# A fused attention and mixture-of-experts kernel whose start-up is re-ordered: q loaded before k and v, the next batch's keys made earlier, one table loaded sooner

## The chip, the cores and the metric

The kernel runs on one core of a Trainium2 chip. The metric is the device time of one execution in microseconds (us). Executions of one kernel differ by 2 to 3 us out of 990, and that matters here: the whole effect is about 3 us. *Times* come from four to six executions of a kernel (three for the first reading of the kernel before), beside the kernel before on the same chip. *Milestones* come from one profiled execution: they tell where TensorE is at which moment, to a hundredth of a microsecond, but of one execution only.

Engines: PE is TensorE, DVE is VectorE, ACT is ScalarE, POOL is GpSimd, SP the queue engine.

## The reference, cut to what matters

A cosine-weighted linear attention for 8 batches of 576 tokens (8 heads of 64) feeds a mixture of 8 experts with Sinkhorn routing.

```python
q_p, k_p = phi(q), phi(k)                    # relu, times cos and sin of the position: 64 -> 128 features
kv = einsum('bhsf,bhsd->bhfd', k_p, v)       # "key sums"
z = sum(k_p, axis=2)
out = einsum('bhsf,bhfd->bhsd', q_p, kv) / (einsum('bhsf,bhf->bhs', q_p, z) + 1e-6)
# x = out as [4608, 512]; P = sinkhorn(exp(x @ w_gate)), 8 iterations
# result = sum over experts e of P[:, e] * (relu(x @ w1[e]) @ w2[e])
```

Nearly all the work is the expert layers. They need x, so they cannot start before the attention of the first batch is done. That start-up is the subject.

## The kernel before

One batch of attention goes through these steps, four head pairs (`hk`) at a time: load q, k, v (cast to fp16 on the way, by the one queue that POOL feeds); ReLU of k on ACT (`prep_k`); the products with cos and sin on DVE (`k_p`, `q_p`); transposes of `q_p` on PE, with a ReLU on the way out of PSUM (`turn`); key sums on PE (`sums_begun`) and their copies (`sums_made`, which makes `zsel`); `denominators` (24 matmuls, then add, reciprocal and rounding on DVE); and `attend`, which writes `xT`. From batch 2 on the transposes of `q_p` are made by a DMA. Tokens go through the first expert in blocks of 512: block 0 uses batch 0, block 1 needs batch 1 too.

Engines work strictly in the written order here (a helper chains each instruction to the one before it on its engine), so a late operand holds up everything behind it.

```python
        load(0, 0, "kv")
        # ... ident made on POOL
        load(0, 1, "kv")
        load(0, 0, "q")
        load(0, 1, "q")
        w0 = new_weights(wA)
        load_w1(w0, 0, 4)
        load(1, 0, "kv")
        load(1, 1, "kv")
        load(1, 0, "q")
        load(1, 1, "q")
        load_w2(w0, 0, 4)

        def keep_busy(n):            # dummy matmuls, which keep PE's clock up
            for _ in range(n):
                te.matmul(out=idle_ps[:, 0:P], lhsT=ones_sq[:], rhs=ones_sq[:], start=True, stop=True)
        idle_ps = ps_y.tile([P, Dm], FP32, name="y_ps")
        keep_busy(56)
        # ...
        prep_pair(0, 0)                      # relu(k), k_p, copy of v for head pairs 0 and 1
        begun = [sums_begun(0, 0)]
        keep_busy(12)
        prep_pair(0, 1)
        sums_made(0, 0, begun[0])
        prep_q(0, 0)
        begun.append(sums_begun(0, 1))
        keep_busy(12)
        prep_q(0, 1)
        for hk in range(HK):
            for i in range(3):
                turn(0, hk, i, hk < 2 or i == 0)
            keep_busy(8)
            # ... sums_made(0, 1), prep_q(0, hk + 2)
        denominators(0)
        keep_busy(36)
        # ...
        for hk in range(HK):
            attend(0, hk)
            if hk:
                prep_k(1, hk - 1)
            if hk == HK - 1:
                prep_kv(1, 0)
                prep_kv(1, 1)
                prep_k(1, 3)
            # ... block 0's first four w1 products, as xT comes
        prep_kv(1, 2)
        prep_kv(1, 3)

        ahead = (                            # of batch 2, done in block 0's slots 11 to 15
            (prep_k, 0), (prep_q, 0), (prep_k, 1), (prep_kv, 0), (prep_q, 1), (prep_k, 2),
            (prep_kv, 1), (prep_q, 2), (prep_k, 3), (prep_kv, 2),
        )
                # block 0, by slot: sums of batch 1 in 4 and 6, turns in 7 to 10, denominators in 10,
                # gates in 11, attends in 13, 14, 15, 15
```

A block has 16 slots: 8 for w1 products (four matmuls of 512 columns each), 8 for w2 products.

Of the kernel before, what the change touches and what calls it, by code (L numbers as in the profile page):

```python
# [10 lines left out]
FP32 = mybir.dt.float32  # L11
# [4 lines left out]
AF = mybir.ActivationFunctionType  # L16
# [9 lines left out]
def kernel(  # L26
# [18 lines left out]
    HK = H // 2  # L45
# [74 lines left out]
    def new_weights(pool):  # L120
        return pool.tile([P, KT, F], F16, name="w1e"), pool.tile([P, FT, Dm], F16, name="w2e")

    def load_w1(w, e, cuts):
        view = moe_w1[e].rearrange("(kt p) f -> p kt f", p=P)
        for i in range(cuts):
            f0, f1 = i * F // cuts, (i + 1) * F // cuts
            nc.gpsimd.dma_start(out=w[0][:, :, f0:f1], in_=view[:, :, f0:f1])

# [26 lines left out]
    def ffn2(hT, w, c0, g, y_ps, fts):  # L155

        for ft in fts:
            te.matmul(
                out=y_ps,
                lhsT=hT[:, ft, c0 : c0 + P],  # L160
                rhs=w[1][:, ft, :],
                start=(ft == 0),
                stop=(ft == FT - 1),
            )
        if FT - 1 in fts:

            if g % 2 == 0 or TCH // P <= g < (B - 1) * TCH // P:
                se.copy(out=acc(g), in_=y_ps)
            else:
                ve.tensor_copy(out=acc(g), in_=y_ps)  # L170
# [10 lines left out]
    with ExitStack() as p1:  # L181
# [15 lines left out]
        def load(b, half, names="qkv", held_back=False):  # L197
            for name in names:
                x = ld.tile([P, 2, C, D], F16, name=f"{name}_ld")
                view = sources[name][b].rearrange("(hk hh) (p c) d -> (hh p) hk (c d)", hh=2, c=C)  # L200
                i = nc.gpsimd.dma_start(
                    out=x[:].rearrange("p hk c d -> p hk (c d)"),
                    in_=view[:, 2 * half : 2 * half + 2],
                )
                if held_back:

                    after(ve.last, i)
                for i in range(2):
                    loaded[name, b, 2 * half + i] = x[:, i]
# [8 lines left out]
            allow_small_or_imprecise_dtypes=True,  # L218
        )

        load(0, 0, "kv")
        ones_sq = cs_pool.tile([P, P], F16, name="ones_sq")
        ve.memset(ones_sq[:], 1.0)
        ident = cs_pool.tile([P, P], F16, name="ident")
# [1 line left out]
            out=ident[:], in_=ones_sq[:], pattern=[[-1, P]], compare_op=ALU.is_equal,  # L226
            fill=0.0, base=0, channel_multiplier=1,
        )
        load(0, 1, "kv")
        load(0, 0, "q")  # L230
        load(0, 1, "q")
        w0 = new_weights(wA)
        load_w1(w0, 0, 4)
        load(1, 0, "kv")
        load(1, 1, "kv")
        load(1, 0, "q")
        load(1, 1, "q")
        load_w2(w0, 0, 4)
# [7 lines left out]
                )  # L246

        idle_ps = ps_y.tile([P, Dm], FP32, name="y_ps")
        keep_busy(56)

        wrap = cs_pool.tile([P, C], FP32, name="wrap")
        ve.tensor_scalar(
# [9 lines left out]
        s_b = sval[:].unsqueeze(2).to_broadcast([P, C, D])  # L262
        se.activation(out=cs[:, :, 0, :], in_=s_b, func=AF.Sin, bias=half_pi[:], scale=-ang)
        se.activation(out=cs[:, :, 1, :], in_=s_b, func=AF.Sin, scale=ang)


        zmask = held[:, C * 2 * D + 3 * H * D : C * 2 * D + 3 * H * D + H * 32].rearrange("p (h r) -> p h r", h=H)
# [76 lines left out]
                qps[b, hk] = q_p  # L344

        def prep_kv(b, hk, copy=ve.tensor_copy):
            k16, v16 = (loaded.pop((name, b, hk)) for name in "kv")
            k_p = kp_pool.tile([P, C, 2, D], F16, name="k_p")
            ve.tensor_tensor(
                out=k_p[:], in0=k16.unsqueeze(2).to_broadcast([P, C, 2, D]),  # L350
                in1=cs, op=ALU.mult,
            )

            v_aug = v_augs[(b * HK + hk) % len(v_augs)]
            copy(out=v_aug[:, :, 0:D], in_=v16)
            kps[b, hk] = (k_p, v_aug)

        def turn(b, hk, i, scalar=None):

# [45 lines left out]
        def sums_made(b, half, kv_ps):  # L405
            kv_sb, zsel = kvs[b]
            for hh in range(2):
                kv_v = kv_ps[hh][:, 0 : 2 * (D + 1)].rearrange("p (hk d) -> p hk d", d=D + 1)
                se.copy(out=kv_sb[:, 2 * half : 2 * half + 2, hh, :], in_=kv_v[:, :, 0:D])
                ve.tensor_tensor(  # L410
                    out=zsel[:, 4 * half + hh : 4 * half + 4 : 2, :],
                    in0=zmask[:, 4 * half + hh : 4 * half + 4 : 2, :],
                    in1=kv_v[:, :, D : D + 1].to_broadcast([P, 2, 32]),
                    op=ALU.mult,
                )

        def denominators(b):

# [85 lines left out]
        turns = [(hk, i) for hk in range(HK) for i in range(3)]  # L504


        def prep_pair(b, half):
            for hk in (2 * half, 2 * half + 1):
                prep_k(b, hk)
            for hk in (2 * half, 2 * half + 1):  # L510
                prep_kv(b, hk, se.copy)

        prep_pair(0, 0)
        begun = [sums_begun(0, 0)]
        keep_busy(12)
        prep_pair(0, 1)
        sums_made(0, 0, begun[0])
        prep_q(0, 0)
        begun.append(sums_begun(0, 1))
        keep_busy(12)  # L520
        prep_q(0, 1)
        for hk in range(HK):
            for i in range(3):
                turn(0, hk, i, hk < 2 or i == 0)
            keep_busy(8)
            if hk == 0:
                sums_made(0, 1, begun[1])
            if hk < 2:
                prep_q(0, hk + 2)
        denominators(0)  # L530
        keep_busy(36)

        hT = hA.tile([P, FT, TCH], F16, name="hT")
        first_ps = [
# [3 lines left out]
        ]  # L538
        for hk in range(HK):
            attend(0, hk)  # L540
            if hk:
                prep_k(1, hk - 1)
            if hk == HK - 1:
                prep_kv(1, 0)
                prep_kv(1, 1)
                prep_k(1, 3)
            for kt in ((), (0,), (1,), (2, 3))[hk]:
                for ft, h_ps in enumerate(first_ps):
                    te.matmul(
                        out=h_ps[:],  # L550
                        lhsT=w0[0][:, kt, ft * P : (ft + 1) * P],
                        rhs=xT[:, kt, 0:TCH],
                        start=(kt == 0),
                        stop=(kt == KT - 1),
                    )
                    if kt == KT - 1:
                        se.activation(out=hT[:, ft, 0:TCH], in_=h_ps[:], func=AF.Relu)
        prep_kv(1, 2)
        prep_kv(1, 3)

        ahead = (
            (prep_k, 0), (prep_q, 0), (prep_k, 1), (prep_kv, 0), (prep_q, 1), (prep_k, 2),
# [2 lines left out]
        for j in range(B):  # L565
            b = j + 1
            if j == 0:

                at(0, 4, lambda: begun.append(sums_begun(1, 0)))
                at(0, 5, lambda: sums_made(1, 0, begun[2]))  # L570
                at(0, 6, lambda: begun.append(sums_begun(1, 1)))
                at(0, 7, prep_q, 1, 0)
                at(0, 7, prep_q, 1, 1)
                for hk in range(HK):
                    for i in range(3):
                        at(0, 7 + hk, turn, 1, hk, i)
                    if hk == 0:
                        at(0, 7, lambda: sums_made(1, 1, begun[3]))
                    if hk < 2:
                        at(0, 7 + hk, prep_q, 1, hk + 2)  # L580
                at(0, 10, denominators, 1)
                at(0, 11, gates, 0)
                for hk in range(HK):
                    at(0, min(13 + hk, 15), attend, 1, hk)
            elif b < B:
                if j == 1:
                    at(j, 0, prep_q, b, 3)
                    at(j, 1, prep_kv, b, 3)
                    at(j, 1, sums, b, 0)
                    at(j, 3, sums, b, 1)  # L590
                else:
                    at(j, 0, sums, b, 1)
                at(j, 5 if j == 1 else 3, denominators, b)
                for hk in range(HK):
                    at(j, (8 if j == 1 else 6) + 2 * hk, attend, b, hk)
            if j:
                at(j, 5, gates, j)
            if j == 0:
                for half in range(2):
                    at(j, 3, load, b + 1, half)  # L600
                for i, (fn, hk) in enumerate(ahead):
                    at(j, 11 + i // 2, fn, b + 1, hk)
            elif b + 1 < B:
                for slot, fn, hk in (
                    (3, prep_k, 0), (4, prep_q, 0), (4, prep_k, 1), (5, prep_q, 1),
                    (7, prep_kv, 0), (7, prep_k, 2), (7, prep_q, 2), (9, prep_q, 3),
                    (9, prep_k, 3), (9, prep_kv, 1), (11, prep_kv, 2), (13, prep_kv, 3),
                ):
                    at(j, slot + (j == 1), fn, b + 1, hk)
                at(j, 15 if j == 1 else 14, sums, b + 1, 0)  # L610
            if j == 0:
                for half in range(2):
                    at(1, 0, load, b + 2, half)
            elif b + 2 < B:
                for half in range(2):
                    at(j, 11 + half, load, b + 2, half, "qkv", True)
# [524 lines left out]
```

## Time and profile before

990.26 us, the median of three runs (988.73 to 991.0). The profiled execution has a span of 987.4 us, measured from the first to the last instruction.

| reading of the execution before | us |
|---|---|
| last load of batch 0's v lands | 11.16 |
| last load of batch 0's q lands | 14.91 |
| first transpose of batch 0 | 14.35 |
| denominators of batch 0 start | 20.00 |
| first attend | 23.46 |
| block 1 runs with all its operands (the 4th of its w1 matmuls) | 54.29 |
| block 2 starts | 74.52 |

First the page's busy time of PE and its chain of waits, kernel before. "PE 93%" is the share of the span in which the chain that ended last ran on PE.

```profile
PE 968.0 (98%) x7846; PEld 677.9 (69%) x7846; DVE 810.4 (82%) x1838; ACT 566.4 (57%) x1260; POOL 60.4 (6%) x82
...
PE 93%; DMA 2%; DVE 2%; ACT 1%; POOL 1%; issue 0%; DVEq 0%; POOLq 0%; ACTq 0%; SPq 0%
```

PE is the bound, so only a microsecond in which PE idles, or runs dummies, or runs at a low clock, can be won. They lie in the start-up. Next the windows view, kernel before: in each stretch the busy us of each engine with the number of instructions, then the granted PE clock, the DMA share and GB/s.

```profile
10.00:15.00 5.00, 3.51 (x62) 3.31 (x60) 3.15 (x6) 2.61 (x7) 2.08 (x3) 0.57 1.30 199
45.00:50.00 5.00, 4.26 (x30) 2.14 (x29) 4.93 (x12) 2.80 (x8) 0.00 (x0) 1.00 1.27 201
50.00:55.00 5.00, 3.03 (x18) 1.32 (x18) 4.97 (x12) 2.12 (x6) 0.00 (x0) 1.00 0.84 163
```

From 10 to 15 us the clock is 0.57. From 45 to 55 us DVE is full (4.93 and 4.97 of 5) while PE is busy only 4.26 and 3.03. The timeline of PE says what it waits for; the columns are start, us, engine, line, operation, output and inputs, count, and in brackets the idle time before and what ended it.

```profile
14.35 0.85 PE L109 MATMUL small_ps<-ident,q_p 128*128 128x128 f16 x6
...
20.00 0.89 PE L109 MATMUL small_ps<-q_pT,zsel 128*32 128x192 f16 x24
...
23.46 0.42 PE L109 MATMUL small_ps<-hl,acc_hi 96*128 96x192 f16 x3 [0.45 <-DVE hl L109]
...
51.97 0.61 PE L109 MATMUL h_ps<-xT,w1e 128*128 128x512 f16 x2
53.57 0.38 PE L109 MATMUL h_ps<-xT,w1e 128*128 128x512 f16 x1 [0.99 <-DVE xT L109]
54.29 1.24 PE L109 MATMUL h_ps<-xT,w1e 128*128 128x512 f16 x5 [0.35 <-DVE xT L109]
```

Block 1's w1 matmuls come in the order of `xT`'s four parts. The third waits 0.99 us for an `xT`, the fourth 0.35 us: DVE has other work in front of it. One more line, from ACT's timeline, kernel before:

```profile
41.94 1.28 ACT L109 ACT_TABLE_LOAD   x1
```

This is the Exp table, loaded at its first use, in the middle of the busy part.

### The profile page before, as it was taken

To read this page: it belongs to the slowest core of one execution; us is meant where nothing else is said; L and a number is where in the kernel's file an instruction comes from. 1 tells how busy PE (TensorE), PEld (TensorE's weight loads), DVE (VectorE), ACT (ScalarE), POOL (GpSimd) and SP (SyncE) were. 2 spreads that over 40 slices of the span, in tenths; PEclk is the share of its full clock that TensorE was granted. 3 is DMA by queue.
4 is the path that set the end of the run, shared out by engine and by line. 5 is a ranking of instruction groups with operands and counts; after the bars stand their busy time and mean duration, and the time that the engine had idled before them with its cause. 6 is when DMAs were issued, how large, how long until landed. Compare 5 with 4: busy or idle time off the path is not lost.

```text
span 987.4 us, 20228 instructions
## 1 busy us (share of the span) xinstructions
PE 968.0 (98%) x7846; PEld 677.9 (69%) x7846; DVE 810.4 (82%) x1838; ACT 566.4 (57%) x1260; POOL 60.4 (6%) x82
## 2 busy tenths in 40 slices
PE   7999999989999999999999999999999999999997
PEld 6445544447777777777777777777777777777775
DVE  5886774779889888988789888988789888988887
ACT  5756665467776555555555555555555555555551
POOL 6302110010000000000000000000000000000001
PEclk8999999999999999999999999999999999999999
DMA  9969981642013410133113400233103400104535
GB/s 168 206 99 154 160 153 26 125 67 67 26 48 68 75 42 25 38 79 67 42 33 68 88 29 25 51 66 68 49 25 68 92 25 27 48 25 114 131 86 128
DMA packets 80336, 73.54 MB, mean 74 GB/s; under 512 B 33264, under 2 KB 72176, under 8 KB 80240
## 3 DMA queue, kind: packets, MB, share of 16 engines
q0 software_dynamic: 27232, 30.94, 19.9%
q1 hardware_dynamic: 52768, 41.06, 16.9%
q8 instruction: 61, 1.00, 0.4%
q14 instruction: 35, 0.29, 0.1%
q10 hardware_dynamic: 240, 0.26, 0.1%
HBM read 83.12 MB, written 12.98 MB: 97 GB/s over the span
## 4 chain that ended last, share of the span: by engine, by line
PE 93%; DMA 2%; DVE 2%; ACT 1%; POOL 1%; issue 0%; DVEq 0%; POOLq 0%; ACTq 0%; SPq 0%
PE rows_ps L109 34%; PE h_ps L109 28%; PE copied_ps L109 11%; PE p_ps L109 11%; PE y_ps L109 5%; PE small_ps L109 4%; DMA v_ld<-in_v_dram 2%; DMA q_pT<-q_p 1%; DVE xT L109 0%; DVE acc_hi L814 0%; POOL hs_last L829 0%; DVE P_tok L109 0%; DMA out_dram<-acc_lo 0%; DVE colp L109 0%; ACT u L109 0%
## 5 line engine op out<-in xcount | busy, mean ns | idle before, releaser
L814 DVE SCALAR_TENSOR_TENSOR acc_lo<-rows_ps,P_tok,acc_lo 128x512 f32<-128x512 f32 (+1 forms) x322 | 203.7, 642 | 74.5 <-PE rows_ps L109 74.4
L109 PEld LDWEIGHTS <-H 128*128 128x128 f16 x2080 | 203.0, 98 | 83.1 <-issue 1.2
L750 ACT CAST u<-h_ps 128x384 f16<-128x384 f32 x288 | 137.8, 478 | 131.2 <-PE h_ps L109 130.6
L109 PEld LDWEIGHTS <-w1e 128*128 128x128 f16 x1632 | 156.3, 98 | 67.9 <-issue 7.8
L744 DVE CUSTOM_DVE_ANT_0 H<-p_ps,u 128x384 f16<-128x384 f32 x329 | 181.7, 552 | 6.6 <-PE p_ps L109 6.4
L109 PEld LDWEIGHTS <-hs 128*128 128x128 f16 x1500 | 146.6, 98 | 56.2
L109 PE MATMUL h_ps<-S,w1e 128*128 128x384 f16 x672 | 164.1, 326 | 1.1 <-ACT u L109 0.9
L109 PE MATMUL p_ps<-xT,T 128*128 128x384 f16 x672 | 164.1, 326 | 0.1
L109 PE MATMUL h_ps<-xT,w1e 128*128 128x384 f16 (+1 forms) x616 | 150.3, 351 | 1.4 <-DVE xT L109 1.3
L109 PE MATMUL rows_ps<-V,H 128*128 128x256 f16 x1000 | 150.0, 273 | 0.7 <-DVE acc_hi L814 0.7
L109 PE MATMUL rows_ps<-w2e,hs 128*128 128x256 f16 x1000 | 150.0, 273 | 0.0
L782 ACT ACTIVATE H<-h_ps 128x384 f16<-128x384 f32 x144 | 70.7, 491 | 95.0 <-PE h_ps L109 95.0
L109 PEld LDWEIGHTS <-T 128*128 128x128 f16 x1008 | 98.1, 98 | 29.2 <-issue 2.8
L109 PE MATMUL rows_ps<-w2e,H 128*128 128x256 f16 (+1 forms) x568 | 91.2, 285 | 0.0
L763 ACT COPY copied_ps<-h_ps 128x384 f32<-128x384 f32 x144 | 67.5, 468 | 35.2 <-PE h_ps L109 35.2
L773 ACT ACTIVATE H<-copied_ps 128x384 f16<-128x384 f32 x144 | 70.9, 492 | 20.3 <-PE copied_ps L109 20.3
L109 PE MATMUL h_ps<-S,T 128*128 128x384 f16 x336 | 81.8, 325 | 0.3 <-ACT copied_ps L109 0.3
L109 PE MATMUL copied_ps<-xT,w1e 128*128 128x384 f16 x336 | 82.1, 326 | 0.0
L109 PE MATMUL copied_ps<-w2e,H 128*128 128x256 f16 x504 | 75.5, 272 | 0.0
L109 PE MATMUL rows_ps<-V,hs 128*128 128x256 f16 x500 | 75.0, 272 | 0.0
L814 DVE SCALAR_TENSOR_TENSOR acc_lo<-copied_ps,P_tok,acc_lo 128x256 f32<-128x256 f32 x126 | 60.3, 479 | 0.4
L814 DVE SCALAR_TENSOR_TENSOR acc_hi<-rows_ps,P_tok,acc_hi 128x512 f32<-128x512 f32 (+1 forms) x56 | 41.3, 738 | 20.1 <-PE rows_ps L109 19.3
(135 smaller groups left out, 957.5 us busy)
## 6 DMA issues: line engine op xcount, KB each, us to landing
S<-x_saved SPq DMA_DIRECT2D x108, 192.0 KB, 2.4
out_dram<-acc_lo SPq DMA_DIRECT2D x62, 128.0 KB, 2.4
w1e<-in_moe_w_dram POOLq DMA_DIRECT2D x7, 1024.0 KB, 9.3
w2e<-in_moe_w_dram POOLq DMA_DIRECT2D x7, 1024.0 KB, 10.0
k_ld<-in_k_dram POOLq DMA_DIRECT2D x16, 288.0 KB, 8.4
v_ld<-in_v_dram POOLq DMA_DIRECT2D x16, 288.0 KB, 9.4
q_ld<-in_q_dram POOLq DMA_DIRECT2D x16, 288.0 KB, 7.8
x_saved<-S SPq DMA_DIRECT2D x18, 192.0 KB, 1.9
```

What stands on the lines that cost most here:

```text
L109: i = getattr(self.engine, name)(*args, **kwargs)
L744: latest = ve._custom_dve(TENSOR_ADD_SAT, out=out, in0=ps[:, 0:TU], in1=t[:], s0=FP32_MAX, s1=0.0)
L750: se.copy(out=t[:], in_=ps[:, 0:TU])
L763: se.copy(out=Y[:, 0:TU], in_=X[:, 0:TU])
L773: se.activation(out=h11, in_=Y[:, 0:TU], func=AF.Relu)
L782: se.activation(out=h12, in_=X[:, 0:TU], func=AF.Relu)
L814: ve.scalar_tensor_tensor(out=a, in0=rows, scalar=P_tok[:, g, self.e : self.e + 1], in1=a, op0=ALU.mult, op1=ALU.add,)
```

## The change

Its intent: start the transposes as soon as q is there, so that only the key sums remain when v, the last load, lands; make batch 1's keys between the first attends, so that everything of batch 1 moves one slot up; load the Exp table while ACT waits for the first load. Four more things ride along: w1's second half is loaded after batch 1's k and v, the dummies are re-tuned (148 to 166), the accumulator copies of two odd tiles of block 0 go from DVE to ACT, and in batch 0 the `zsel` products precede the copies of the key sums.

```diff
-            if g % 2 == 0 or TCH // P <= g < (B - 1) * TCH // P:
+            if g % 2 == 0 or g < (B - 1) * TCH // P:
                 se.copy(out=acc(g), in_=y_ps)
...
-        load(0, 0, "kv")
+        load(0, 0, "q")
...
-        load(0, 1, "kv")
-        load(0, 0, "q")
         load(0, 1, "q")
+        for name in "kv":
+            load(0, 0, name)
+            load(0, 1, name)
         w0 = new_weights(wA)
-        load_w1(w0, 0, 4)
+        load_w1(w0, 0, 4, (0, 1))
         load(1, 0, "kv")
         load(1, 1, "kv")
+        load_w1(w0, 0, 4, (2, 3))
...
-        keep_busy(56)
+        keep_busy(80)
...
+        early = cs_pool.tile([P, 1], FP32, name="early")
+        se.activation(out=early[:], in_=half_pi[:], func=AF.Exp)
...
-        prep_pair(0, 0)
-        begun = [sums_begun(0, 0)]
-        keep_busy(12)
...      (the front shown above)
+        begun = []
+        for hk in range(HK):
+            prep_q(0, hk)
+            for i in range(3):
+                turn(0, hk, i, hk < 2 or i != 1)
+        for hk in range(HK):
+            prep_k(0, hk)
+            prep_kp(0, hk)
+        keep_busy(30)
+        for half in range(2):
+            prep_v(0, 2 * half, se.copy)
+            prep_v(0, 2 * half + 1, ve.tensor_copy)
+            begun.append(sums_begun(0, half))
+            keep_busy((16, 6)[half])
         sums_made(0, 0, begun[0])
+        sums_made(0, 1, begun[1])
         denominators(0)
-        keep_busy(36)
+        keep_busy(34)
...
             attend(0, hk)
-            if hk:
-                prep_k(1, hk - 1)
-            if hk == HK - 1:
-                prep_kv(1, 0)
-                prep_kv(1, 1)
-                prep_k(1, 3)
+            prep_k(1, hk)
+            prep_kp(1, hk)
+            if hk >= 2:
+                prep_v(1, hk - 2, se.copy)
...
-        prep_kv(1, 2)
-        prep_kv(1, 3)
+        prep_v(1, 2, se.copy)
+        prep_v(1, 3, ve.tensor_copy)
...      (batch 1 in block 0: second key sums from slot 6 to 5, turns from 7-10 to 6-9,
...       denominators from 10 to 9, gates from 11 to 10, attends from 13, 14, 15, 15 to 12, 13, 14, 15)
```

More of the change, by code (lines that the diff above doesn't have):

```diff
@@ L121, in new_weights, with load_w1 @@
         return pool.tile([P, KT, F], F16, name="w1e"), pool.tile([P, FT, Dm], F16, name="w2e")
-    def load_w1(w, e, cuts):
+    def load_w1(w, e, cuts, parts=None):
         view = moe_w1[e].rearrange("(kt p) f -> p kt f", p=P)
-        for i in range(cuts):
+        for i in range(cuts) if parts is None else parts:
             f0, f1 = i * F // cuts, (i + 1) * F // cuts
@@ L346, in prep_kv, with prep_kp @@
         def prep_kv(b, hk, copy=ve.tensor_copy):
-            k16, v16 = (loaded.pop((name, b, hk)) for name in "kv")
+            prep_kp(b, hk)
+            prep_v(b, hk, copy)
+        def prep_kp(b, hk):
+            k16 = loaded.pop(("k", b, hk))
             k_p = kp_pool.tile([P, C, 2, D], F16, name="k_p")
@@ L352, in prep_kv, with prep_v @@
             )
-            v_aug = v_augs[(b * HK + hk) % len(v_augs)]
-            copy(out=v_aug[:, :, 0:D], in_=v16)
-            kps[b, hk] = (k_p, v_aug)
+            kps[b, hk] = (k_p, v_augs[(b * HK + hk) % len(v_augs)])
+        def prep_v(b, hk, copy):
+            copy(out=kps[b, hk][1][:, :, 0:D], in_=loaded.pop(("v", b, hk)))
         def turn(b, hk, i, scalar=None):
@@ L408, in sums_made, with values @@
                 kv_v = kv_ps[hh][:, 0 : 2 * (D + 1)].rearrange("p (hk d) -> p hk d", d=D + 1)
-                se.copy(out=kv_sb[:, 2 * half : 2 * half + 2, hh, :], in_=kv_v[:, :, 0:D])
+                def values():
+                    se.copy(out=kv_sb[:, 2 * half : 2 * half + 2, hh, :], in_=kv_v[:, :, 0:D])
+                if b:
+                    values()
                 ve.tensor_tensor(
@@ L415, in sums_made @@
                 )
+                if not b:
+                    values()
         def denominators(b):
@@ L504 @@
         turns = [(hk, i) for hk in range(HK) for i in range(3)]
-        def prep_pair(b, half):
-            for hk in (2 * half, 2 * half + 1):
-                prep_k(b, hk)
-            for hk in (2 * half, 2 * half + 1):
-                prep_kv(b, hk, se.copy)
-        prep_pair(0, 0)
-        begun = [sums_begun(0, 0)]
-        keep_busy(12)
-        prep_pair(0, 1)
-        sums_made(0, 0, begun[0])
-        prep_q(0, 0)
-        begun.append(sums_begun(0, 1))
-        keep_busy(12)
-        prep_q(0, 1)
-        for hk in range(HK):
-            for i in range(3):
-                turn(0, hk, i, hk < 2 or i == 0)
-            keep_busy(8)
-            if hk == 0:
-                sums_made(0, 1, begun[1])
-            if hk < 2:
-                prep_q(0, hk + 2)
+        begun = []
[12 more added lines that the diff above has]
+            keep_busy((16, 6)[half])
+        sums_made(0, 0, begun[0])
+        sums_made(0, 1, begun[1])
         denominators(0)
-        keep_busy(36)
+        keep_busy(34)
         hT = hA.tile([P, FT, TCH], F16, name="hT")
@@ L570 @@
                 at(0, 5, lambda: sums_made(1, 0, begun[2]))
-                at(0, 6, lambda: begun.append(sums_begun(1, 1)))
-                at(0, 7, prep_q, 1, 0)
-                at(0, 7, prep_q, 1, 1)
+                at(0, 5, lambda: begun.append(sums_begun(1, 1)))
+                at(0, 6, prep_q, 1, 0)
+                at(0, 6, lambda: sums_made(1, 1, begun[3]))
+                at(0, 6, prep_q, 1, 1)
                 for hk in range(HK):
                     for i in range(3):
-                        at(0, 7 + hk, turn, 1, hk, i)
-                    if hk == 0:
-                        at(0, 7, lambda: sums_made(1, 1, begun[3]))
+                        at(0, 6 + hk, turn, 1, hk, i)
                     if hk < 2:
-                        at(0, 7 + hk, prep_q, 1, hk + 2)
-                at(0, 10, denominators, 1)
-                at(0, 11, gates, 0)
+                        at(0, 6 + hk, prep_q, 1, hk + 2)
+                at(0, 9, denominators, 1)
+                at(0, 10, gates, 0)
                 for hk in range(HK):
-                    at(0, min(13 + hk, 15), attend, 1, hk)
+                    at(0, 12 + hk, attend, 1, hk)
             elif b < B:
```

## The prediction

> **What bounds the kernel.** TensorE: the page has PE busy 968.0 of 987.4 us (98%) and 93% of the chain of waits. From about 76 us on the timeline shows PE without a gap, and the change alters nothing there. What is at stake is the ramp before the second token block's matmuls run (54.29 us): some 12 us at most, so 2% (20 us) is out of reach.
>
> **The ramp before** (timeline, landings).
> - Batch 0's six loads land 1.43 us apart: k 6.44, v 7.87, k 9.67, v 11.16, q 12.58, q 14.91 us. Transposes start at 14.35, denominators at 20.00, the first attend at 23.46.
> - From there to 54.29 is 30.8 us. The PE work in it, by the timeline's start-to-start times (64 expert matmuls of 0.217, eight attends of 0.71, 36 transposes of 0.055, key sums 2x0.68, denominators 0.84, gates 0.4), is about 25 us: 6 lost. Of these 3.6 fall in 45.5 to 54.3 us, where DVE is full (windows: 4.93 and 4.97 of 5) and PE waits for xT.
> - The Exp table load, 1.28 us, sits on ACT at 41.94.
>
> **What changes.**
> 1. q lands first (6.4, 7.9), v last (12.6, then 14 to 15). Transposes start near 7.3, but the denominators now hang on v and a full ACT: ten q_pT copies of 0.435 from 7.5, four key ReLUs and two v copies of 0.63 end at 15.6; DVE ends its last k_p and v copies near 16. Then sums 0.7, 16 dummies 0.9, sums 0.7, zsel 0.4: denominators near 18.9 instead of 20.0. Gain 1.1 (0 to 2). The +18 dummies lie in here. The clock record has half clock from 10.74 to 17.57 us; the Trainium skill ("TensorE: Matmul & The Clock Gate", What's actually happening) says activity releases the throttle and idleness brings it back; this trace agrees (PE idle 4.4 us between 5.7 and 11.9). Some of that stretch may go.
> 2. Between the first attends ACT gets a key ReLU each (0.66), and two v copies: loss 0.4.
> 3. Batch 1's keys are ready earlier; its sums, turns, denominators and attends move up a slot: a 0.73 us gap at 36 us goes, and another group of four expert matmuls (0.87) runs behind the reciprocal. Gain 1.5.
> 4. Two accumulator copies (0.68 each) go from DVE to ACT where DVE is full; ACT has lost its table load there, which moves to the start, where ACT idles until 6.46. Gain 0.8.
> 5. w1's second half lands about 24 to 25 us instead of 18.2 to 19.6; needed near 30, so nothing lost. w2 lands as before.
>
> Sum 3.0 us. Nothing gives it back later, since PE is saturated after 76 us.
>
> **Predicted: 987.0 us**, range 984.2 to 989.4. Faster by over 2%: 0.005; within 2%: 0.99; slower: 0.005.
>
> **What would show it.** Right: denominators(0) at 18 to 19.5 us; first attend near 22.3; second block's matmuls at 50.5 to 52; the same group means after that; the second table load before 6 us, none at 42; PE idle in 45 to 55 below 2.7 us. Wrong: denominators at 20 or later (ACT queue, cold clock); DVE full and PE idle as long before the second block (the early gain turned into waiting there); w1 or batch 1 loads ending a PE wait.
>
> **What would make it wrong.** Half clock lasting through key sums and dummies (+1); denominators at 17 us, or the DVE-full stretch disappearing (-3); run noise (2.3 us over three runs).

## The result and the profile after

The changed kernel took 986.84 us (median of four runs, 986.34 to 988.33), the kernel before 990.63 (median of four, 988.73 to 991.24). The ratio is 0.9967, with a 95% interval of 0.995 to 0.9985. Ratios here are the mean time of one kernel's fast runs over that of the other's of the same rounds, so not quite the ratio of the medians. Over all, the changed kernel has 13 fast runs with a mean of 987.45 us, the kernel before 44 with a mean of 990.06: a gain of 2.6 us, 0.26%.

The same views of the changed kernel: the page, then the windows.

```profile
PE 969.7 (98%) x7864; PEld 678.5 (69%) x7864; DVE 808.1 (82%) x1833; ACT 568.1 (58%) x1266; POOL 60.4 (6%) x82
...
PE 93%; DVE 3%; ACT 1%; DMA 1%; issue 1%; POOL 0%; DVEq 0%; ACTq 0%; SPq 0%; POOLq 0%
```

```profile
10.00:15.00 5.00, 3.96 (x39) 3.88 (x40) 3.23 (x6) 4.01 (x9) 2.19 (x3) 0.66 1.28 200
45.00:50.00 5.00, 4.88 (x33) 2.31 (x32) 4.94 (x12) 4.18 (x11) 0.00 (x0) 1.00 1.21 202
50.00:55.00 5.00, 3.38 (x42) 1.68 (x42) 4.57 (x10) 1.42 (x4) 0.00 (x0) 0.68 1.12 180
```

PE's idle time from 45 to 55 us fell from 2.71 us (10 less 4.26 and 3.03) to 1.74. The 0.68 in the clock column of 50 to 55 us is new, and will matter. The timeline of PE, changed kernel:

```profile
6.95 1.62 PE L109 MATMUL small_ps<-ident,q_p 128*128 128x128 f16 x18
...
18.76 0.84 PE L109 MATMUL small_ps<-q_pT,zsel 128*32 128x192 f16 x24
...
22.18 0.42 PE L109 MATMUL small_ps<-hl,acc_hi 96*128 96x192 f16 x3 [0.58 <-DVE hl L109]
...
49.06 0.82 PE L109 MATMUL h_ps<-xT,w1e 128*128 128x512 f16 x3
51.62 2.19 PE L109 MATMUL h_ps<-xT,w1e 128*128 128x512 f16 x5 [1.74 <-DVE xT L109]
53.75 1.17 PE L109 MATMUL small_ps<-acc_lo,k_p 64*128 64x65 f16 x36
```

Transposes begin 7.4 us earlier, denominators 1.24 us earlier, block 1's fourth matmul 2.67 us earlier. But the wait before it has become a single one of 1.74 us, and the five matmuls after it take 2.19 us where before they took 1.24: the trace's clock record has half clock from 51.76 to 55.17 us in this execution. Last, ACT's timeline of the front, changed kernel:

```profile
3.45 1.28 ACT L109 ACT_TABLE_LOAD   x1
...
7.32 3.17 ACT L109 ACTIVATE q_pT<-small_ps 128x384 f16<-128x384 f32 x8 [2.37 <-PE small_ps L109]
11.33 1.13 ACT L109 ACTIVATE q_pT<-small_ps 128x384 f16<-128x384 f32 x2 [0.84 <-PE small_ps L109]
12.36 2.39 ACT L109 ACTIVATE k_ld<-k_ld 128x576 f16<-128x576 f16 x4
14.65 1.23 ACT L109 COPY acc_lo<-v_ld 128x576 f16<-128x576 f16 x2
```

The table load is where ACT had nothing else to do. From 7.32 us on ACT has one gap of 0.84 us until its v copies end at 15.88, 0.9 us after the last v load landed (14.98): ACT rather than the load is what the front seems to hang on, which a run below tests.

The two profiled spans differ by only 0.8 us (987.4 and 986.6), although the times differ by 3. The ledger of that, from when PE reaches the same matmul in both executions (before minus after):

```
milestone                          before    after    gained so far
denominators of batch 0             20.00    18.76        1.24
block 1, 4th w1 matmul              54.29    51.62        2.67
block 1, first w2 product           63.49    62.34        1.15      half clock: -1.52
block 2 starts                      74.52    72.90        1.62      a wait of 0.29 us of before is gone
block 3 starts                      94.16    93.09        1.07      a wait of 0.46 us at 89 us
last matmul                        983.19   982.36        0.83
```

So the profiled execution of the changed kernel is one of its slower ones (988.33 us, 0.9 over its mean), and half clock is why; that of the kernel before is one of its faster ones (989.15 us, 0.9 under its mean). The experiments had to settle which part of the change gains what, and how much of the times is the clock.

### The profile page after: what moved, and what is told of

Same layout as the page of the kernel before. It is cut to its first block, busy times and chain, and to the rows that moved or that the text cites. A ratio compares the mean times of both kernels' runs of the same rounds, so it can differ in the third digit from the quotient of the medians.

```text
span 986.6 us, 20264 instructions
## 1 busy us (share of the span) xinstructions
PE 969.7 (98%) x7864; PEld 678.5 (69%) x7864; DVE 808.1 (82%) x1833; ACT 568.1 (58%) x1266; POOL 60.4 (6%) x82
## 4 chain that ended last, share of the span: by engine, by line
PE 93%; DVE 3%; ACT 1%; DMA 1%; issue 1%; POOL 0%; DVEq 0%; ACTq 0%; SPq 0%; POOLq 0%
PE rows_ps L109 34%; PE h_ps L109 28%; PE copied_ps L109 11%; PE p_ps L109 11%; PE y_ps L109 5%; PE small_ps L109 4%; DMA q_pT<-q_p 1%; DVE k_p L109 0%; DVE xT L109 0%; DVE acc_hi L819 0%; POOL hs_last L834 0%; DVE P_tok L109 0%; DMA out_dram<-acc_lo 0%; ACT q_pT L109 0%; DVE colp L109 0%
```

## The experiments

The parts are compared from a common zero, the start of batch 0's denominators, because what comes before jitters with the landing of the loads, and what comes after does not: in the twelve fast profiled executions with full clock there the time from it to the first attend is 3.42 to 3.53 us (4.05 in the one with half clock).

### Control: the changed kernel again

No edit.

> The changed kernel unaltered, to learn its spread. The first profiled run of it showed half clock from 51.8 to 55.2 us (clock 0.997, span 986.6) while two later runs had clock 0.998 and 1.000 and spans 984.7 and 984.6. If these half-clock windows make the spread, runs with clock 0.997 lie near 987 to 988 us and runs with 0.998 or more near 986.3; ratio to before about 0.9965 (0.995 to 0.998). If the spread is something else, time and clock do not go together.

Measured: 988.1 us median of five, the slow one included; fast runs 986.39, 986.59, 988.1 and 988.41; ratio 0.9973 (0.996 to 0.9987). The profiled execution: 1675.46 us at a clock of 0.557. Its windows view:

```profile
5.00:10.00 5.00, 5.00 (x55) 4.87 (x54) 2.18 (x3) 0.28 (x1) 4.27 (x6) 0.63 1.08 157
500.00:505.00 5.00, 5.00 (x23) 2.80 (x21) 1.74 (x4) 1.79 (x4) 0.00 (x0) 0.56 0.00 0
```

From 5.8 us to the end the clock stayed at 0.56. It happened once in all the runs, and is left out of every comparison. Time and mean clock did not go together as expected: 986.39 and 988.41 both had 0.998. A mean over 986 us cannot tell a half-clock window that hurts from one that falls on dummies.

### Only more dummies, on the kernel before

```diff
-        keep_busy(56)
+        keep_busy(80)
...
         begun = [sums_begun(0, 0)]
-        keep_busy(12)
+        keep_busy(30)
```

> The kernel before with only more dummy matmuls at the start (80 for 56, and 30 for the first 12). Theory A (the load order and the earlier transposes win the front): the half-clock window from 10.7 us may shorten, and denominators come at 19.4 to 20 us, time within 0.6 us of before. Rival B (the change wins the front by its dummies, which keep the clock up): denominators at 18.7 to 19.1 us as in the changed kernel, time 1 to 1.5 us under before.

Measured: 989.75 us, ratio 0.9991 (0.9978 to 1.0005). PE's clock was 1.00 in every window up to 50 us, so the dummies did what they are for, and the denominators still came at 19.94 us:

```profile
19.94 0.89 PE L109 MATMUL small_ps<-q_pT,zsel 128*32 128x192 f16 x24
```

So the denominators came when theory A said, but that does not refute the rival (the front is won by the dummies), because in this execution the loads landed up to 1.3 us later than in the profile before (second load 9.16 against 7.87 us, last v 12.28 against 11.16). Counted from the last v landing, the denominators came after 7.66 us here and after 8.84 in the kernel before. The later-part run below, on the same chip, has the old front with loads as late (second load 8.67, last v 12.19 us) at half clock, and its denominators at 20.64. So full clock is worth some 0.7 us in that old front. The front-only run, also on this chip, comes at 19.40, 1.24 us before the later-part run. By mean times the dummies alone gain 0.55 us and the front-only run 0.93, with intervals that overlap. So perhaps half of the front's gain, or more, could be had by dummies alone; the milestones are of single executions, and how the gain divides between the clock and the order of the loads stays open.

### Only the front

The changed kernel with these parts put back: keys of batch 1 late, slots late, no early Exp, two odd copies on DVE.

```diff
-            prep_k(1, hk)
-            prep_kp(1, hk)
-            ...
+            if hk:
+                prep_k(1, hk - 1)
+            ...                       (and the slots, the table and the copies as before)
```

> The changed kernel's load order, early transposes and dummies; from the first attends on as in the kernel before (keys late, slots late, Exp table loaded at its first use, odd copies on DVE). Theory: denominators at 18.8 us, and the gain of 1.2 us is kept to the second block, whose matmuls then run at about 53.1 instead of 54.3 us; time 1.0 to 1.5 us under before. Rival (the later stage is paced by DVE or by the loads of batch 1, which now land 1 to 2 us later): the gain shrinks below 0.5 us by the second block.

Measured: 989.05 us, ratio 0.9989 (0.9976 to 1.0001), a mean of 0.9 us under before. Denominators at 19.40, because the second load landed at 8.77 instead of 8.13 us. From there to block 1's fourth matmul it took 34.26 us, as the kernel before (34.30). So the front's gain is kept until there, and the rival falls. The line answers to the one at 54.29 us of the kernel before:

```profile
53.66 1.24 PE L109 MATMUL h_ps<-xT,w1e 128*128 128x512 f16 x5 [0.35 <-DVE xT L109]
```

Of the front's own parts only the dummies were run singly; the order of the `zsel` products and the later w1 load were not.

### Only the later part

```diff
         (the front of the kernel before)
+            prep_k(1, hk)
+            prep_kp(1, hk)
+            ...                       (slots, early Exp and copies as in the change)
```

> The front of the kernel before with the later part of the change (keys of batch 1 between the attends, slots one up, Exp table up front, odd copies on ACT). Theory: denominators at 20.0 us; second block's matmuls at about 52.9 us (1.4 us gained); time 1 to 2 us under before, more if no half-clock window follows the wait before the second block. Rival (the parts only work together): under 0.5 us gained.

Measured: 988.55 us, ratio 0.9987 (0.9975 to 1.0), a mean of 1.1 us under before. Denominators at 20.64 us (late loads, half clock), and from there to block 1's fourth matmul 32.92 us against 34.30: 1.38 us gained, and 1.43 in the whole change (32.87). Half clock followed this wait too (53.86 to 57.27 us), so the five matmuls behind it are slow:

```profile
53.56 2.04 PE L109 MATMUL h_ps<-xT,w1e 128*128 128x512 f16 x5 [1.74 <-DVE xT L109]
```

The two halves add: by milestones independently of each other, by mean times 0.9 + 1.1 = 2.0 us, where the control gained 2.5, within the intervals.

### Without the early Exp

```diff
-        early = cs_pool.tile([P, 1], FP32, name="early")
-        se.activation(out=early[:], in_=half_pi[:], func=AF.Exp)
```

> The changed kernel without the early Exp: its table (1.28 us) is loaded at its first use again, near 40 us. Theory as predicted (the load is hidden or worth a few tenths, because ACT idles 1.75 us there while it waits for TensorE): second block's first four matmuls end their wait at the same 32.9 us after the denominators, time within 0.5 us of the changed kernel. Rival (ACT is the pace-maker of that stretch): 0.8 to 1.3 us later.

Measured: 989.08 us, ratio 0.9988 (0.9976 to 1.0001). Denominators to block 1's fourth matmul: 33.46 us instead of 32.87. ACT's timeline of this run:

```profile
41.39 0.59 ACT L109 COPY acc_lo<-y_ps 128x512 f32<-128x512 f32 x1 [1.75 <-PE y_ps L109]
41.99 1.28 ACT L109 ACT_TABLE_LOAD   x1
43.28 0.20 ACT L109 ACTIVATE P_tok<-small_ps 128x32 f32<-128x32 f32 x1
43.38 0.58 ACT L109 COPY acc_lo<-y_ps 128x512 f32<-128x512 f32 x1
```

Of the 1.28 us of the load, 0.59 reached PE, more than the few tenths I expected of it and less than the rival's 0.8 to 1.3. The idleness that I counted on (1.75 us before the copy at 41.39) is there, but the table load comes after it: its place in the written order is behind that copy. Neither theory was quite right. Where an engine works in the written order, as here, idle time hides only what stands next in that order.

### The two odd copies back on DVE

```diff
-            if g % 2 == 0 or g < (B - 1) * TCH // P:
+            if g % 2 == 0 or TCH // P <= g < (B - 1) * TCH // P:
```

> The changed kernel with the two odd accumulator copies of the first block back on DVE. Theory (DVE is full from 45 to 52 us and holds back the last xT): denominators to the second block's fourth matmul 33.9 to 34.3 us instead of 32.9, so 1.0 to 1.4 us later, time 1 us over the changed kernel. Rival (ACT's copies of rb hold xT back instead): no change or earlier.

Measured: 988.66 us, ratio 0.9986 (0.9974 to 0.9998). Denominators to block 1's fourth matmul: 33.55 us, 0.68 later than 32.87. That is one copy of 0.68, not two, and less than the 1.0 to 1.4 I wrote down. The wait before block 1 is longer:

```profile
54.16 2.29 PE L109 MATMUL h_ps<-xT,w1e 128*128 128x512 f16 x5 [2.10 <-DVE xT L109]
```

DVE's order of work before the last `xT` is the limit of that stage, as the theory says: what is taken from DVE arrives at PE. In this run half clock fell on 16.5 to 19.9 us, over the key sums and dummies, and the denominators came at 20.61; it fell again on 54.05 to 57.47 us, right behind the wait, which is why these five matmuls took 2.29 us.

### The wait before block 1 filled with dummies

```diff
+            if j == 1:
+                fill_ps = ps_s.tile([P, 512], FP32, name="small_ps")
+                for _ in range(24):
+                    te.matmul(out=fill_ps[:, 0:P], lhsT=ones_sq[:], rhs=ones_sq[:], start=True, stop=True)
             for slot in range(NS):
```

> The changed kernel with 24 dummy matmuls (1.3 us) put into TensorE's wait before the second block. It removes no wait. If the half-clock window after that wait (51.8 to 55.2 us in its first profile) is what costs 1.2 us in some executions and splits the times into 986.4 and 988.2, then here no half clock from 50 to 60 us, second block starts at the same time, and the times gather at 986.3 to 986.8 (spread under 1 us). Rival (the split comes from when the loads land): the spread stays near 2 us.

Measured: 988.27 us, 986.14 to 989.0, ratio 0.9977 (0.9965 to 0.9989). In the profile the wait is full of dummies, the matmuls behind it run at full speed, and block 1 reaches its first w2 product 42.08 us after the denominators, against 43.58 in the changed kernel's first profile, which had half clock there: 1.50 us, the price of one such window. (That the dummies prevented it is not shown: a later profile of the unfilled kernel had none either.)

```profile
50.28 1.50 PE L109 MATMUL small_ps<-ones_sq 128*128 128x128 f16 x24 [0.30 <-ACT rb L109]
51.61 2.10 PE L109 MATMUL h_ps<-xT,w1e 128*128 128x512 f16 x8
53.65 0.75 PE L109 MATMUL small_ps<-acc_lo,k_p 64*128 64x65 f16 x36
```

But the spread stayed, nearly 3 us. The prediction of this run, that the times would gather, failed. The half clock behind the wait costs 1.5 us where it occurs, but it is not the only thing that spreads the times. The front does too, by the landing of the second load and by where a half-clock window falls in it: in the seven fast profiled executions with this front the denominators came at 18.76, 19.40, 18.62, 20.61, 19.59, 18.86 and 20.94 us (and 16.56 to 17.99 in the versions below, which alter it). The two latest, 20.61 and 20.94, had half clock from 16.5 and 17.0 us, over the key sums.

### The last `xT` put first

```diff
-                    at(j, 11 + i // 2, fn, b + 1, hk)
+                    at(j, 11 + i // 2 if i < 6 else 15, fn, b + 1, hk)
```

Batch 2's work of slot 14 goes behind batch 1's last attend.

> The changed kernel with the third batch's preparation of slot 14 (a key product, a copy and a query product, 2.3 us of DVE) put behind the last xT of batch 1. Theory (the wait of 1.74 us before the second block is DVE's order of work): the wait shrinks to under 0.4 us, second block's fourth matmul 31.2 to 31.6 us after the denominators instead of 32.9, no half clock there, time 1.5 to 2.5 us under the changed kernel, about 985. Rival (the last xT waits for ACT or the postponed work stalls the third batch's key sums): the wait is passed on to slot 1 to 3 of the second block, gain under 0.5 us.

Measured: 986.28 us, 986.13 to 986.74, ratio 0.9962 (0.9949 to 0.9975). It is the steadiest version, and no half clock shows in its profile before the end. The fourth matmul came 31.53 us after the denominators, as the theory said, but part of the rival holds too: a new wait follows, for batch 2's key sums:

```profile
50.40 1.24 PE L109 MATMUL h_ps<-xT,w1e 128*128 128x512 f16 x5 [0.40 <-DVE xT L109]
...
55.51 0.46 PE L109 MATMUL small_ps<-acc_lo,k_p 64*128 64x65 f16 x18 [0.97 <-DVE acc_lo L109]
```

0.97 us of the 1.34 won were passed on there. By block 2 almost nothing is left of it: block 2 starts 52.45 us after the denominators here, 52.65 in the run with the dummies, and 52.64 in the third run of the changed kernel below, which had no half clock there either. So most of what it gains over the changed kernel's first profile (54.15) is the absence of half clock behind the wait, which fits the shorter wait but is not shown to come from it. Why its front too was spared the half clock in four of five runs (clock 1.000) these runs do not tell: its front is the changed kernel's, instruction for instruction.

### ReLUs of the first keys on DVE

On top of the last `xT` put first:

```diff
+        prep_q(0, 0)
         for hk in range(HK):
-            prep_q(0, hk)
+            if hk < 3:
+                prep_q(0, hk + 1)
+            else:
+                relu_on_dve(0)            # tensor_scalar max with 0 instead of ACT's Relu
+                prep_kp(0, 0)
             for i in range(3):
                 turn(0, hk, i, hk < 2 or i != 1)
+        relu_on_dve(1)
+        prep_kp(0, 1)
+        ...                               (the other two on ACT; a third v copy on ACT)
-            keep_busy((16, 6)[half])
+            keep_busy((4, 6)[half])
```

> The version with the last xT first, and in the front: each query product made one head pair earlier, two of batch 0's four key ReLUs on DVE (0.30 us each by the query ReLUs of the trace, against 0.60 on ACT), one more v copy on ACT, 4 dummies instead of 16 between the key sums. Theory: the denominators of batch 0 wait for a full ACT (6.40 us from the first key ReLU to the denominators in every profile with full clock), not for the loads; they then come at 16.8 to 17.5 us instead of 18.6 to 19.6, and 1.2 to 2 us are gained to the end: about 984.5 us. Rival (the last v load, landing at 14.7 to 15 us, or the chain behind it sets them): 18.3 us or later, gain under 0.5 us.

Measured: the denominators came at 16.56 us, 2.3 us earlier, so the front did not hang on the last v load (14.70 us here, 14.77 before). Not all of it is ACT's: the chain of the trace has the dummies between the key sums in it, 1.00 us for sixteen in the version before and 0.33 for four here, so 0.67 of the 2.3 us are dummies taken out. (In the third run of the changed kernel half clock fell on the sixteen, and they took 1.82 us.) The other 1.6 us come from ReLUs and a v copy moved between ACT and DVE and from the earlier query products, which this run does not separate; in the version before, the last link ahead of the key sums was DVE's v copy, behind four key products that had waited for ACT's first ReLU. Yet the time was 986.98 us (986.13 to 987.73), ratio 0.997 (0.9957 to 0.9982): nothing gained on the version before (986.28, on another chip). PE's timeline, then DVE's, of this run:

```profile
16.56 0.84 PE L109 MATMUL small_ps<-q_pT,zsel 128*32 128x192 f16 x24
...
48.09 1.24 PE L109 MATMUL h_ps<-xT,w1e 128*128 128x512 f16 x5 [0.40 <-DVE xT L109]
...
55.28 0.46 PE L109 MATMUL small_ps<-acc_lo,k_p 64*128 64x65 f16 x18 [3.05 <-DVE acc_lo L109]
```

```profile
51.03 0.30 DVE L109 TENSOR_SCALAR q_ld<-q_ld 128x576 f16<-128x576 f16 x1
53.44 0.76 DVE L109 TENSOR_TENSOR q_p<-q_ld,acc_hi 128x1152 f16<-128x1152 f16 x1 [2.11 <-DMA q_pT<-q_p]
54.12 0.75 DVE L109 TENSOR_TENSOR k_p<-k_ld,acc_hi 128x1152 f16<-128x1152 f16 x1
54.79 0.45 DVE L109 COPY acc_lo<-v_ld 128x576 f16<-128x576 f16 x1
```

The 2.3 us are there until block 1 (48.09 against 50.40 us), and are lost in one wait of 3.05 us. The key sums came at 55.28 us, in the version before it at 55.51: the same moment, whatever the front did. DVE waited 2.11 us for a DMA transpose of an earlier query product to give its buffer back. That transpose was issued at 41.96 and landed at 53.35 us, just after the last load of batch 3 (53.06).

### All of these, and more work moved off DVE

On top of the last one: batch 1's first two query products made while DVE idles (3.5 us at 30 to 33 us in the changed kernel), two v copies of batch 2 on ACT.

```diff
-                at(0, 6, prep_q, 1, 0)
-                at(0, 6, prep_q, 1, 1)
+        prep_q(1, 0)                      # before block 0's slots
+        prep_q(1, 1)
```

> As the run with ReLUs on DVE, and batch 1's first two query products made in DVE's 3.5 us of idleness before its key sums' diagonals, and two v copies of the third batch on ACT instead of DVE. Theory: the 0.6 us of waits before batch 1's transposes go, and the 0.97 us wait of the third batch's key sums (passed on by putting the last xT first) goes too: 0.8 to 1.5 us less than the run with ReLUs on DVE, about 983.5 us. Rival: the waits move to the next stage again and under 0.4 us remains.

Measured: 987.79 us (986.4 to 989.76), ratio 0.9978 (0.9965 to 0.9991), no better. Half clock fell on 16.8 to 20.2 us in the profile, the denominators came at 17.99, and block 2 started at 71.50 us, where the version before had 71.34. The rival is right.

### The changed kernel a third time

No edit.

> The changed kernel once more beside the two improved ones on the same chip: 986.3 to 988.5 us in two clusters, ratio to before 0.997. In its profile the denominators to the second block's fourth matmul take 32.87 us as in the first; whether half clock follows is open.

Measured: 988.26 us (986.77 to 988.66), ratio 0.9976 (0.9964 to 0.9988). Two clusters again: 986.77 and 986.79, and 988.26 to 988.66. In this profile the half clock fell on 17.0 to 20.4 us and none on the wait before block 1. The line answers to the one at 51.62 us of the first profile after:

```profile
51.26 0.82 PE L109 MATMUL h_ps<-xT,w1e 128*128 128x512 f16 x3
53.82 1.24 PE L109 MATMUL h_ps<-xT,w1e 128*128 128x512 f16 x5 [1.74 <-DVE xT L109]
54.99 0.74 PE L109 MATMUL small_ps<-acc_lo,k_p 64*128 64x65 f16 x36
```

The same wait of 1.74 us, and 1.24 us for the five matmuls instead of 2.19. So the wait belongs to the kernel; the half clock behind it comes and goes from one execution to the next.

### Batch 2's last query product put last

On top of the ReLUs on DVE:

```diff
-                    at(j, 0, prep_q, b, 3)
-                    at(j, 1, prep_kv, b, 3)
+                    at(j, 0, prep_kv, b, 3)
+                    at(j, 2, prep_q, b, 3)
```

> The version with ReLUs on DVE, whose front gain of 2.3 us was lost again in a 3.05 us wait of TensorE at 55.28 us, with one more move: the third batch's last query product goes behind that batch's last key product and v copy on DVE. Theory: DVE works in order, and that query product waited 2.11 us for a DMA transpose to give its buffer back (landed 53.35, behind the loads of batch 3, the last of which lands at 53.06), holding up key product and v copy behind it, so that the key sums came at the same 55.3 us in three versions with denominators from 16.6 to 18.9 us. Then the wait at 55 us is gone or under 0.5 us, the third block starts at 68.5 to 69.5 us (from denominators at 16.6) instead of 71.34, and the time is 983.5 to 985 us, below every version so far. Rival (the loads or transposes set the pace of the next stage as well): the third block starts at 71 us again, or a new wait for a transpose of 1 us or more comes before 75 us, and the time stays near 986 us.

Measured: 987.05 us (985.98 to 988.58), ratio 0.9974 (0.996 to 0.9987). The wait at 55 us went, as the theory said, and three waits for the transposes themselves came in its place, as the rival said:

```profile
56.02 0.34 PE L109 MATMUL small_ps<-q_pT,zsel 128*32 128x192 f16 x6 [1.11 <-DMA q_pT<-q_p]
56.94 0.35 PE L109 MATMUL small_ps<-q_pT,zsel 128*32 128x192 f16 x6 [0.57 <-DMA q_pT<-q_p]
57.84 0.35 PE L109 MATMUL small_ps<-q_pT,zsel 128*32 128x192 f16 x6 [0.55 <-DMA q_pT<-q_p]
```

Block 2 started at 71.15 us. With the denominators of batch 0 at 18.86, 16.56, 17.99 and 16.72 us, the four versions with the last `xT` first start it at 71.31, 71.34, 71.50 and 71.15. That looks like a floor. In three of the four the waits name the DMA transposes (DVE waited 2.11 and 0.89 us for one, PE 1.11, 0.57 and 0.55); in the one with only the last `xT` first, DVE was busy without a gap from 50.3 us to the key sums, so its 0.97 us are DVE's own work. Packets that started in each microsecond, by queue, counted from the trace of the run with the ReLUs on DVE:

```
us             44    47    49    51    52    53    56
loads         188   145   144    69    18     0     0
transposes      0   144   151   306   553  1051  1149
```

From 47 to 50 us, beside the loads, the transposes get one packet for each packet of a load, though their packets are of about 250 bytes and the loads' of about 1100; alone they move seven times as many. The Trainium skill ("DMA: Bandwidth & Descriptors", Queues, rings and completion order) says that each DMA engine takes turns between the queues it has work for, packet by packet; the counts agree, if the trace's packets are what the page calls so. By these counts batch 3's loads, which nothing needs before block 2, hold up batch 2's transposes, which block 1 waits for. That is argued, not shown by a run, and it is not the whole: from 54 to 55 us only 152 packets of transposes started, with no load left. To issue those loads later, or to let PE make batch 2's transposes: whether that lowers the floor is open.

## Why the prediction was right, point by point

The predicted time was 987.0 us; measured were 986.84 in the first four runs, and 987.45 as the mean of 13. The bound, the ceiling and the place of the gain were right: everything happens in the start-up, in which PE was idle or waiting. Several terms of the sum were mis-sized, with opposite signs, and that they nearly cancelled is luck: at block 1 the gain was 2.67 us (1.24 and 1.43) for a predicted 3.0, though one term was short by 1.3. (One reading in it is loose: the six loads of the kernel before landed 1.42 to 2.33 us apart, not 1.43 throughout.)

| step of the prediction | predicted | measured | by |
|---|---|---|---|
| 1: front | gain 1.1, denominators 18.9 | 1.24, at 18.76 | first profiles; 18.62 to 20.94 over seven |
| 2: ReLUs between the attends | loss 0.4 | loss 0.08 or none | block 0's slot 4 starts 10.82 us after the denominators, before 10.74 (10.70 to 10.81 in three profiles of that code) |
| 3: slots one up | gain 1.5 | 0.16 (0.24 if the loss of step 2 is real) | what is left of 1.43 |
| 4: two copies and table load | gain 0.8 | 0.68 + 0.59 | two runs that undo them |
| 5: w1's second half later | 0 | 0 | no PE wait for w1 in the profile |
| block 1's 4th w1 matmul ("second block's matmuls") | 50.5 to 52 us | 51.62 | first profile |
| "nothing gives it back later" | 0 | 1.5 in some executions | half clock after the wait |

- **Step 1.** The path was right: ACT's row of copies and ReLUs, predicted to end at 15.6 us, ended at 15.88, DVE's last v copy near 16.6 (predicted near 16), and the sixteen dummies stood in the chain for 1.00 us, as the sum had them (0.9). Relieving ACT and taking out twelve dummies moved the denominators by 2.3 us. How much of the gain over the kernel before is the load order and how much the clock stays open (the run with only more dummies). Not expected was the jitter of this front from one execution to the next.
- **Step 3 is the term that was wrong.** I counted a group of four expert matmuls that would run behind the reciprocal, and a gap of 0.73 us that would vanish. The gap was only cut up: two waits, 0.29 and 0.30 us, stand in its place at 34 to 35 us. And what runs behind the reciprocal is worth nothing while DVE's row of work before the last `xT` paces the stage; it shows up as a longer wait at its end (1.74 us in one piece, where there were 0.99 and 0.35). The 0.16 is by subtraction, not by a run of its own, and assumes that the parts add.
- **Step 4** was too small by 0.47: the table load cost 0.59 us and the copies 0.68, together 1.27 for a predicted 0.8. This and the 0.3 to 0.4 of step 2 made up for some 0.8 of the 1.3 us that step 3 lacked.
- **"Nothing gives it back later"** is the sentence that failed. A wait of PE can be followed by 3.4 us of half clock, which costs 1.5 us. The kernel before can have it too: with more dummies in front it showed one from 53.4 us. It is one reason why single executions of either kernel lie 2 us apart; the front is another. In the changed kernel and its variants it followed the wait in four of the five profiles in which that wait was 1.74 us or more. PE was not quite saturated after 76 us either: it waits for 1.20 us at 206.69 before and at 205.61 after, but there the two kernels wait alike.

A version that beats both is not established. With the last `xT` put first the mean of five runs is 986.34 us, 1.1 us under the 13 runs of the changed kernel, but the intervals of the ratios to the kernel before (0.9949 to 0.9975, and 0.995 to 0.9985) overlap.

## What to carry to other kernels

- A gain in a start-up is kept only up to the next thing that runs by its own clock. Here a front 2.3 us faster was lost whole in one wait that ended with DMA transposes, which, by the packet counts though not by a run, shared the DMA engines with loads not yet needed; before speeding up a stage, ask when the transfers of the stage after it land, and which loads they share the engines with.
- On an engine that works in written order, work for later placed before the operand that is needed now is a wait for somebody else. One reordering of DVE's work took 1.34 us from a wait, of which 0.97 came back as the next one; and of a table load of 1.28 us that stood behind ACT's idle time in the order, 0.59 reached PE.
- When an effect is as small as the spread, compare milestones from a common zero within the traces (they repeat to 0.1 us here where the clock is full), and use times only to confirm. Look at the clock record before explaining a difference between two single profiles.

## What the Trainium skill lacked or had wrong

- "TensorE: Matmul & The Clock Gate" (What's actually happening) has windows of about 3.4 us that do not start with the kernel. The runs agree: every half-clock stretch in the start-ups of the fast profiles was 3.41 or 6.83 us long, and one and the same program had it behind the same 1.74 us wait in one execution and not in another. Its rule to avoid idle gaps of PE over some 3.4 us (HAM oscillation) is no guarantee here: a wait of 1.74 us was followed by half clock in three profiles, of the changed kernel, of its later part alone and of it without the early Exp, and one of 2.10 us with the two odd copies back on DVE, at 1.5 us each. What decides stays open: in the 3.41 us just before the half clock PE was idle for 1.74 to 2.14 us in these four, and for 1.43 in the kernel before with more dummies, but in the third run of the changed kernel a stretch as long, counted from the last change of the clock, held the same 1.74 us and none followed.
- The same page knows a half clock, a limit of 13/16 and a clock stuck at a quarter for 50 us; none of them is a core that keeps 0.56 for a whole execution under dense matmuls: 1675.46 us at 0.557, once.
- "ScalarE: Activation LUTs" (What ACT_TABLE_LOAD costs) gives about 1283 ns for the load and about 1380 ns of draining. The load was 1.28 us here as well; no draining shows: the copy before the load ended at 41.98 us, the load began at 41.99, and the next activation 1.29 us later. PE felt 0.59 us of it.
- "DMA: Bandwidth & Descriptors" says that queues take turns by packets, but not what it does to a DMA transpose beside large loads: 8.7 to 11.4 us from issue to landing for batch 2's first (in the changed kernel, and with the ReLUs on DVE or the last query product put last), where the same transpose took 5.29 in the kernel before, and the median of all its transposes is 3.4.
